# Fewer and larger loads near the end of a decode step: 29 load transfers in place of 37

## The chip, the cores and the metric

The kernel runs on one core of one Trainium2 chip. Its time is the device time of one execution in microseconds (us). The engines are named as in the profile: PE is TensorE (PEld its weight loads), DVE is VectorE, ACT is ScalarE, POOL is GpSimd, SP is SyncE, whose queue issues the loads.

## The reference: what is computed

One decode step of a transformer block for a single token, with modulated layer norms (`c` gives shifts, scales and gates), attention over a cache, and a feed-forward part with ReLU. Cut to what matters:

```python
D, Hq, Hkv, Sk, Dh, Dff = 512, 32, 8, 32768, 128, 1792       # bf16, one token
sa, ca, ga, sb, cb, gb = split(silu(c) @ w_mod, 6)
h = layernorm(x) * (1 + ca) + sa
q = h @ wq                                  # 32 query heads, 4 for each of 8 cached heads
p = softmax(q @ k.T / sqrt(Dh))             # over 32768 keys of each cached head
x = x + ga * ((p @ v) @ wo)
h = layernorm(x) * (1 + cb) + sb
out = x + gb * (relu(h @ w1) @ w2)
```

K and V of one cached head are 8 MiB each; eight heads make 128 MiB, all read once. The weights add wm (3 MiB), wq (4), wo (4), w1 and w2 (1.75 each).

## The kernel before, in words

**The stream.** All large loads go out on SP's queue, in the order of the list `stream`; `need(key)` issues the loads of the list up to the one that is wanted, and `load` makes one transfer of each entry. A load of K or V of head g is called Kg or Vg. Each is cut along the keys into four steps (0 to 3); a "half" is two steps. The order before is: half of K0, wm, wq, the other half of K0, then K1, V0, K2, V1, K3, V2, K4, V3, K5, V4 whole; K6 and V5 in halves; K7a, V6a, K7b, V6b (a and b are the first and the second half); V7 as a half and two quarters; wo in four pieces (`WOP`: four heads, two, one, one); w1 whole; w2 in five pieces (`W2P`). The second half of K0 is cut unevenly into three transfers (`UNEVEN`): 128 rows without their last 256 elements, and those 256 elements of 111 and of 17 rows.

**Room.** SBUF has a ring of three slots of 8 MiB each. A load takes the slot of the load three places back, so its issue waits until that one has been used: V6 for the scores of K6, V7 for PV of V5, wo and all that follows (`tail_sb`) for the scores of K7. SP's queue is in order: a load that waits holds up all behind it. Each transfer also waits for the one eight places before it, which used the same semaphore.

**One head.** For head h, `turn_k` transposes K on DVE in 32x32 blocks, `scores` multiplies it with the block-diagonal queries (`qbd`, 64 matmuls of 512 columns), and `softmax`, a generator that is advanced step by step with `next`, takes the maximum (DVE, PE), the exponentials (ACT), a transpose of P (DVE) and the sums (PE). `pv` multiplies P with V (64 matmuls of 512 columns, 16 a step), `blocks` (DVE), `o_cols` (PE) and `normalise` (DVE) bring the result into columns.

**The order of work.** PE and DVE follow the program's order (`manual_schedule`). In turn h of the loop stand the scores of head h, its softmax, and PV of head h-1. For heads 0 to 4 PV is a loop on PE; for later heads (`HALVED`) it is unrolled, and half of it may run before the softmax. Behind the loop comes head 7, written out by hand.

**The tail.** `spread(i)` lays the head outputs of piece i of wo out for `project(i)`. The first two pieces are multiplied row by row (`WOROWS`): one-row matmuls of 512 columns into `a_rows`, which `join_rows` turns into columns. The last two, of one head each, are multiplied as columns (L605). `keep_clock(n)` puts n matmuls in between whose result is not used. Then come the second layer norm (`layernorm_T`, whose result is `h2T`), w1 (L765), ReLU, w2 (L788), two DVE steps and the store.

`SPACE` is a number of drain instructions that SP executes after V0's load.

Of the kernel before, what the change touches and what calls it, by code (L numbers as in the profile page):

```python
# [17 lines left out]
def kernel(  # L18
# [25 lines left out]
    NTILE = Sk // (P * TK)  # L44
    NG = NTILE // 2

    WOP = [(0, Hkv // 2), (Hkv // 2, Hkv // 4), (Hkv - 2, 1), (Hkv - 1, 1)]
    WOROWS = 2
    LAST = Hkv - 1
    LOOPED = Hkv - 2  # L50
    HALVED = LOOPED - 1
    W2P = [(0, 5), (5, 10), (10, 12), (12, 13), (13, 14)]
    W1P = [(0, KT)]

    OUT0, OUT1 = 30, 34

    UNEVEN, EDGE, MOST = ("k", 0, (2, 3)), 2 * TK * Dh - D // 2, 111
    SPACE = 14
    assert Dh == 128 and REP == 4 and D == 512 and FT == W2P[-1][1] and NTILE == 4
    scale = float(Dh) ** -0.5  # L60
    eps = 1e-5
# [50 lines left out]
    def load(key):  # L112
        kind = key[0]
        if kind == "wm":
            t = piece("wmq_sb", 0, WM).rearrange("p (kt n) -> p kt n", kt=KT)
            src = wm_v
        elif kind == "wq":
            t = piece("wmq_sb", WM, WQ).rearrange("p (kt n) -> p kt n", kt=KT)
            src = wq_v
        elif kind in "kv":  # L120
            g, steps = key[1], key[2]
            src = (kv if kind == "k" else vv)[g, :, TK * steps[0]:TK * (steps[-1] + 1), :]
            name = f"Ksb{g}" if kind == "k" else f"Vsb{g}"
            t = piece(name, TK * Dh * steps[0], TK * Dh * len(steps)).rearrange("p (j d) -> p j d", d=Dh)
        elif kind == "wo":
            g0, n = WOP[key[1]]
            t = piece("tail_sb", g0 * REP * D, n * REP * D).rearrange("p (r d) -> p r d", d=D)
            src = wo_v(key[1])
        elif kind == "w1":
            k0, k1 = W1P[key[1]]  # L130
            t = piece("tail_sb", WO + k0 * Dff, (k1 - k0) * Dff).rearrange("p (kt f) -> p kt f", f=Dff)
            src = w1_v[:, k0:k1]
        else:
            f0, f1 = W2P[key[1]]
            t = piece("tail_sb", WO + KT * Dff + f0 * D, (f1 - f0) * D).rearrange("p (f d) -> p f d", d=D)
            src = w2_v[:, f0:f1]
        if key == UNEVEN:
            row, src_row = (x.rearrange("p j d -> p (j d)") for x in (t, src))
            for rows, cols in (
                (slice(0, P), slice(0, EDGE)), (slice(0, MOST), slice(EDGE, None)), (slice(MOST, P), slice(EDGE, None)),  # L140
            ):
                stream_dma(row[rows, cols], src_row[rows, cols])
        else:
            stream_dma(t, src)
        if key[:2] == ("v", 0):
            for _ in range(SPACE):
                nc.sync.drain()
        if kind in "kv":
            for i, u in enumerate(steps):
                loaded[(kind, g, u)] = t[:, TK * i:TK * (i + 1), :]  # L150
        else:
            loaded[key] = t

    def stream_dma(dst, src):
        i = nc.sync.dma_start(out=dst, in_=src)  # L155
        tc.stamp_issue_order_token(i.ins, "sp_stream")
        if last_loop:

            tc.add_manual_dep(i.ins, last_loop[0], mybir.DependencyInfo(
                mybir.DependencyClass.NoSync, mybir.DependencyReason.DATA))  # L160
# [1 line left out]
    whole, halves = [(0, 1, 2, 3)], [(0, 1), (2, 3)]  # L162
    stream = [("k", 0, halves[0]), ("wm",), ("wq",), ("k", 0, halves[1])]
    for g in range(LOOPED):
        stream += [("k", g + 1, s) for s in (halves if g >= HALVED else whole)] + [("v", g, s) for s in (halves if g >= HALVED else whole)]
    for s in halves:
        stream += [("k", LAST, s), ("v", LOOPED, s)]
    stream += [("v", LAST, (0, 1)), ("v", LAST, (2,)), ("v", LAST, (3,))] + [("wo", i) for i in range(len(WOP))]
    stream += [("w1", i) for i in range(len(W1P))] + [("w2", i) for i in range(len(W2P))]
    pos = [0]  # L170

# [71 lines left out]
    pick8 = const.tile([16, 8], BF16)  # L243
    nc.vector.tensor_tensor(out=pick8[:], in0=ident_bf[0:16, 0:8], in1=ident_bf[0:16, 8:16], op=ALU.add)
    cx_sel = const.tile([16, 2], BF16)
    nc.vector.tensor_copy(out=cx_sel[:], in_=cmask[8][0:16, 0:2])
    cx_bd = piece("wmq_sb", R0 + 2048 + 4 * P, D)[0:16].rearrange("p (b n) -> p b n", b=8)
    nc.vector.tensor_tensor(  # L248
        out=cx_bd, in0=cx_row[:].unsqueeze(1).to_broadcast([16, 8, D // 8]),
# [23 lines left out]
    def row_bank(t):  # L273

        nc.vector.memset(t, 0.0)
        return t
# [282 lines left out]
    def o_cols(g):  # L559
        nc.tensor.matmul(  # L560
            oT_ps[:, REP * g:REP * (g + 1)], lhsT=Y_tiles.pop(g)[:], rhs=qsel,
            start=True, stop=True, skip_group_check=True,
        )

    def part_of(g):
        return [i for i, (g0, n) in enumerate(WOP) if g0 <= g < g0 + n][0]

# [25 lines left out]
    def project(i):  # L593

        n = WOP[i][1] * REP
        wo_sb = need(("wo", i))
        for r in range(n):
            if i < WOROWS:
                nc.tensor.matmul(
                    a_rows[0][32 * (r % 4):32 * (r % 4) + 1, :], lhsT=o2_tiles[i][:, r:r + 1],  # L600
                    rhs=wo_sb[:, r, :], start=False, stop=(i == WOROWS - 1 and r >= n - 4), skip_group_check=True,
                )
                continue
            for ko in range(KT):
                nc.tensor.matmul(  # L605
                    attnT_ps[:, ko:ko + 1],
                    lhsT=wo_sb[:, r, :].rearrange("p (m ko) -> p ko m", ko=KT)[:, ko, :],
                    rhs=o2_tiles[i][:, r:r + 1], start=False, stop=(i == len(WOP) - 1 and r == n - 1),
                    skip_group_check=True,
                )  # L610

    a_rows = []

    def join_rows():

        aT = room("tail_sb", TAIL, [P, 512])
        nc.vector.transpose(
            out=aT.rearrange("p (a ko m) -> p a ko m", a=4, ko=KT),
            in_=a_rows[0].rearrange("p (a m ko) -> p a ko m", a=4, ko=KT),
        )  # L620
        for a in range(4):
            nc.tensor.matmul(
                attnT_ps[32 * a:32 * a + 32, :], lhsT=place32[:],
                rhs=aT.rearrange("p (a ko m) -> p a ko m", a=4, ko=KT)[:, a, :, 0],
                start=False, stop=False, skip_group_check=True,
            )

    spare = []
# [8 lines left out]
    with tc.manual_schedule(engines={mybir.EngineType.PE, mybir.EngineType.DVE}):  # L637
# [9 lines left out]
        for g in range(LOOPED):  # L647
            h = g + 1
            build_qbd(h)
            for u in range(NTILE):  # L650
                for half in range(2):
                    turn_k(h, u, half)
                    scores(h, u, half)
                if soft and u == 1:
                    next(soft, None)
            if g - 1 in [sum(w) for w in WOP]:
                spread(part_of(g - 2))
            if g >= HALVED:
                pv(g, (0, 1))
            soft = softmax(h)  # L660
            next(soft)
            if g > 0:
                blocks(g - 1)
            next(soft)
            if g > 0:
                o_cols(g - 1)
            next(soft)
            next(soft)
            pv(g, (2, 3) if g >= HALVED else (0, 1, 2, 3))
            if g > 0:  # L670
                normalise(g - 1)
            next(soft)
            open_o(h)
            next(soft)
        g, h = LOOPED, LAST
        build_qbd(h)
        turn_k(h, 0, 0)
        turn_k(h, 0, 1)
        next(soft, None)
        turn_k(h, 1, 0)  # L680
        turn_k(h, 1, 1)
        blocks(g - 1)
        scores(h, 0, 0)
        scores(h, 0, 1)
        scores(h, 1, 0)
        o_cols(g - 1)
        scores(h, 1, 1)
        normalise(g - 1)
        spread(part_of(g - 1))
        bank_max(h, 0)  # L690
        pv(g, (0, 1))
        for u in (2, 3):
            for half in range(2):
                turn_k(h, u, half)
                scores(h, u, half)
        bank_max(h, 1)
        soft = softmax(h)
        next(soft)
        next(soft)
        next(soft)  # L700
        pv(g, (2,), range(6))
        next(soft)
        next(soft)
        open_o(LAST)
        pv(g, (2,), range(6, 16))
        pv(g, (3,))
        next(soft)
        next(soft, None)
        end_b.append(two_banks("end_ps"))
        a_rows.append(row_bank(end_b[0][:, 0, :]))  # L710
        blocks(g)
        pv(LAST, (0, 1))
        o_cols(LAST - 1)
        normalise(LAST - 1)
        pv(LAST, (2,))
        spread(2)
        hid_ps = ps_o.tile([P, 512], F32, tag="o", name="hid_ps")
        nc.vector.memset(hid_ps[:], 0.0)
        pv(LAST, (3,))
# [3 lines left out]
        project(0)  # L723
        keep_clock(2)
        o_cols(LAST)
        keep_clock(2)
        project(1)
        normalise(LAST)
        spread(3)
        keep_clock(2)  # L730
        project(2)
        keep_clock(1)
        join_rows()
        keep_clock(1)
        project(3)


        stat2 = const.tile([P, 2], F32)
# [88 lines left out]
```

## Time and profile before

| | us |
|---|---|
| median of 3 runs | 354.13 (354.13 to 354.36) |
| the profiled execution | 354.42 |
| its span, first to last instruction | 352.6 |
| PE busy | 272.3 |
| DVE busy | 195.6 |
| mean load rate over the span | 424 GB/s |

In the profile a row of a timeline gives the start of a run of like instructions in us from the span's start, its length, the engine, the line of the kernel, the operation, what it writes and reads, how many there were, and in brackets how long the engine was idle before and what it waited for. A row of windows gives a stretch, its length, then busy time and number of instructions of PE, PEld, DVE, ACT and POOL, then PE's granted clock (1.00 is full), the share of the 16 DMA engines in use, and GB/s. A row of DMA issues gives how many transfers, their size, and the median time in us from issue to landing. The DMA queue of the loads is q1; its row has packets, MB and the share of the span of 16 engines.

### The profile page before, as it was taken

Reading aid. Unit: us, or ns where it says so; the run is one execution under the profiler, and the core shown is the slowest. Engines: PE = TensorE matmul, PEld = TensorE weight load, DVE = VectorE, ACT = ScalarE, POOL = GpSimd, SP = SyncE. Lnnn points to the kernel's source line nnn. Section 1 sums busy time; section 2 is a strip of 40 time slices with the busy share of each in tenths; the row PEclk is TensorE's granted clock in tenths of the full one; section 3 lists DMA queues with packets and bytes.
Section 4 is the critical chain, followed back from the end, with each engine's and each line's share of the span. In section 5 each row is a group of like instructions: output and inputs, shape, how many; then the busy total and the mean of one; then the engine's idle time right before and its main releaser. Section 6 shows DMA issues by size and latency. Waiting matters only on the chain. (4 is left out here: it accounts for less than half of the span.)

```text
span 352.6 us, 3544 instructions
## 1 busy us (share of the span) xinstructions
PE 272.3 (77%) x1310; PEld 111.8 (32%) x1310; DVE 195.6 (55%) x167; ACT 18.7 (5%) x37; POOL 6.0 (2%) x26
## 2 busy tenths in 40 slices
PE   0054980695999679884988499976999999789994
PEld 0021330232333224331333233322444443234442
DVE  7662563983079513965099316956674293743142
ACT  1200003001000010001000100001000100011000
POOL 3000000000000000000000000000000000000000
PEclk9996895698999969998999979996999999999999
DMA  8999989999999999999999999999999999999995
GB/s 353 404 432 456 468 387 461 446 401 446 439 424 440 416 439 446 401 455 446 409 453 446 409 453 431 426 394 439 446 414 427 450 429 424 431 453 398 432 426 213
DMA packets 5222, 149.57 MB, mean 424 GB/s; under 512 B 604, under 2 KB 988, under 8 KB 1628
## 3 DMA queue, kind: packets, MB, share of 16 engines
q1 hardware_dynamic: 5180, 149.43, 98.5%
q8 instruction: 8, 0.13, 0.1%
q14 instruction: 2, 0.02, 0.0%
q10 hardware_dynamic: 32, 0.00, 0.0%
HBM read 149.42 MB, written 0.00 MB: 424 GB/s over the span
## 5 line engine op out<-in xcount | busy, mean ns | idle before, releaser
L441 DVE STREAM_TRANSPOSE Ksb<-Ksb 128x4096 f32<-128x4096 f32 (+1 forms) x34 | 131.5, 3912 | 57.6 <-DMA Ksb<-in_A_k_cache_dram 57.6
L460 PE MATMUL S_ps<-Ksb,qbd 128*128 128x512 bf16 x512 | 118.9, 385 | 19.2 <-DVE Ksb L441 18.3
L523 PE MATMUL o_ps<-Vsb,P_g 128*16 (+1 forms) x512 | 124.3, 401 | 10.9 <-ACT P_g L497 10.0
L460 PEld LDWEIGHTS <-qbd 128*128 128x128 bf16 x512 | 49.2, 97 | 84.9 <-issue 27.6
L523 PEld LDWEIGHTS o_ps<-Vsb,P_g 128*16 x320 | 30.4, 95 | 60.0 <-issue 31.8
L523 PEld LDWEIGHTS <-P_g 128*16 128x16 bf16 x192 | 16.7, 90 | 22.9 <-issue 0.4
L473 DVE TENSOR_REDUCE m_p<-S_ps 128x1 f32<-128x1024 f32 x7 | 8.6, 1223 | 21.8 <-PE S_ps L460 21.8
L502 DVE STREAM_TRANSPOSE P_g<-P_g 128x1024 bf16<-128x1024 bf16 x8 | 10.0, 1245 | 15.6 <-ACT P_g L497 15.6
L494 ACT ACTIVATE nbias<-Mb_ps 128x1 f32<-128x1 f32 x8 | 1.4, 171 | 269.5 <-PE Mb_ps L492 269.5
L324 PE MATMUL mod_ps<-wmq_sb,siluT 128*1 128x512 bf16 x24 | 3.6, 624 | 9.9 <-DMA wmq_sb<-in_w_mod_dram 9.9
L332 DVE STREAM_TRANSPOSE Ksb<-Ksb 128x4096 f32<-128x4096 f32 x2 | 8.8, 4424 | 1.7 <-DMA Ksb<-in_A_k_cache_dram 1.7
L478 PE MATMUL mT_ps<-ident_f,m_p 128*1 128x128 f32 x8 | 2.2, 270 | 8.9 <-DVE m_p L473 7.9
L497 ACT ACTIVATE P_g<-S_ps,nbias 128x1024 bf16<-128x1024 f32 x8 | 8.9, 1114 | 0.2
L560 PE MATMUL acc_ps<-mask_sb,Y 16*128 16x4 f32 x16 | 3.4, 282 | 5.1 <-DVE Y L556 5.1
L552 DVE SCALAR_TENSOR_TENSOR o_ps<-o_ps,Linv,smask 16x512 f32<-16x512 f32 x8 | 5.8, 720 | 2.8 <-PE o_ps L523 2.8
L254 PE MATMUL xc_ps<-cx_sel,wmq_sb 16*128 16x2 bf16 x4 | 0.3, 172 | 8.7 <-DVE wmq_sb L248 8.7
L590 DVE CAST o_sb<-o_ps 128x4 bf16<-128x4 f32 (+2 forms) x4 | 0.7, 167 | 11.1 <-PE o_ps L586 11.1
L415 POOL TENSOR_TENSOR qbd<-qrep_sb,rowpick 128x64 bf16<-128x64 bf16 x8 | 2.4, 299 | 228.0 <-PE S_ps L460 198.3
L509 DVE RECIPROCAL Linv<-L_ps 16x1 f32<-16x1 f32 x8 | 1.0, 126 | 8.3 <-PE L_ps L506 8.3
L556 DVE TENSOR_REDUCE Y<-o_ps 16x128 f32<-16x512 f32 x8 | 5.4, 679 | 0.3
L635 PE MATMUL spare_ps<-qbd,ident_bf 128*128 128x512 bf16 x18 | 5.4, 381 | 0.0
L396 PE MATMUL q_ps<-wmq_sb,hT 128*1 128x512 bf16 x32 | 3.6, 626 | 2.3 <-DMA wmq_sb<-in_A_wq_dram 2.3
(114 smaller groups left out, 71.6 us busy)
## 6 DMA issues: line engine op xcount, KB each, us to landing
Ksb<-in_A_k_cache_dram SPq DMA_DIRECT2D x5, 4096.0 KB, 22.9
Vsb<-in_A_v_cache_dram SPq DMA_DIRECT2D x5, 4096.0 KB, 36.5
wmq_sb<-in_A_wq_dram SPq DMA_DIRECT2D x1, 4096.0 KB, 28.1
Vsb<-in_A_v_cache_dram SPq DMA_DIRECT2D x2, 2048.0 KB, 41.1
Ksb<-in_A_k_cache_dram SPq DMA_DIRECT2D x1, 4032.0 KB, 37.2
wmq_sb<-in_w_mod_dram SPq DMA_DIRECT2D x1, 3072.0 KB, 18.9
tail_sb<-in_A_wo_dram SPq DMA_DIRECT2D x1, 2048.0 KB, 23.2
tail_sb<-in_B_w_dram SPq DMA_DIRECT2D x1, 1792.0 KB, 30.6
```

The lines of the kernel that those rows point to most:

```text
L324: nc.tensor.matmul(dst[j // 4][32 * (j % 4):32 * (j % 4) + 1, :], lhsT=src_T[:, kt:kt + 1], rhs=w[:, kt, j * 512:(j + 1) * 512], start=(kt ...
L332: nc.vector.transpose(out=t, in_=t)
L396: nc.tensor.matmul(q_ps[i][32 * a:32 * a + 1, :].rearrange("o (h e) -> o h e", e=32), lhsT=hT[:, kt:kt + 1], rhs=wq_f[:, kt, i, a], start= ...
L441: t = nc.vector.transpose(out=KTt.bitcast(F32), in_=KTt.bitcast(F32))
L460: nc.tensor.matmul(S_ps_tiles[g], lhsT=qbd[g % 2][:, hp, 4 * (7 - s):4 * (7 - s) + P], rhs=KTv[:, 16 * sl:16 * sl + 16, h, :, par], start= ...
L473: behind_loop(nc.vector.reduce_max(out=m_p[:], in_=S_g.rearrange("p g f -> p (g f)"), axis=AX.X))
L497: nc.scalar.activation(out=P_g[:], in_=S_g.rearrange("p g f -> p (g f)"), func=ACT.Exp, bias=nbias[:], scale=scale, accum_out=l_g[:],)
L502: behind_loop(nc.vector.transpose(out=P_g[:], in_=P_g[:]))
L523: nc.tensor.matmul(o_tiles[g][:], lhsT=PT, rhs=Vx, start=first, stop=False, skip_group_check=True)
L552: nc.vector.scalar_tensor_tensor(out=o, in0=o, scalar=Linv_tiles.pop(g)[:], in1=smask[:].unsqueeze(2).to_broadcast([16, 4, Dh]), op0=ALU.m ...
L556: nc.vector.tensor_reduce(out=Y[:], in_=o.rearrange("p s d -> p d s"), op=ALU.add, axis=AX.X)
L635: nc.tensor.matmul(spare[0], lhsT=ident_bf[:], rhs=qbd[0][:, :, 0:P], start=True, stop=True)
```

## The change

- K0's second half is one transfer again (`UNEVEN`, `EDGE`, `MOST` are gone). SP executes four drains more after V0's load; in front of it two transfers are gone and two waits.
- K6 and V5 are loaded whole. After them come K7a, K7b, V6a, V6b, V7a, V7b, all halves.
- `build_qbd` of head 7 and the transposes of K7a move into the last turn of the loop, ahead of the transpose of head 6's P. Head 7's scores then come in one go, before any PV of head 6, and all PV of V6 comes behind them. `spread` of heads 4 and 5 falls away there.
- wo has two pieces of four heads, both multiplied by rows. So `spread` and `project` of the last four heads come after the last head's `normalise`, and `join_rows` is the last step of the projection. There are eight unused matmuls in this stretch, as before.
- w2 has four pieces: 6, 5, 2 and 1 of 14 instead of 5, 5, 2, 1 and 1.
- `cx_sel`, a small constant at the start, took its values from `cmask[8]`, which is no longer made; it now has a reduction of its own.

PE has 1923 rows of instructions in place of 1975, SP 29 loads in place of 37.

```diff
-    WOP = [(0, Hkv // 2), (Hkv // 2, Hkv // 4), (Hkv - 2, 1), (Hkv - 1, 1)]
-    WOROWS = 2
+    WOP = [(0, Hkv // 2), (Hkv // 2, Hkv // 2)]
-    W2P = [(0, 5), (5, 10), (10, 12), (12, 13), (13, 14)]
+    W2P = [(0, 6), (6, 11), (11, 13), (13, 14)]
-    UNEVEN, EDGE, MOST = ("k", 0, (2, 3)), 2 * TK * Dh - D // 2, 111
-    SPACE = 14
+    SPACE = 18
...
-        if key == UNEVEN:
-            row, src_row = (x.rearrange("p j d -> p (j d)") for x in (t, src))
-            for rows, cols in (
-                (slice(0, P), slice(0, EDGE)), (slice(0, MOST), slice(EDGE, None)), (slice(MOST, P), slice(EDGE, None)),
-            ):
-                stream_dma(row[rows, cols], src_row[rows, cols])
-        else:
-            stream_dma(t, src)
+        stream_dma(t, src)
...
     for g in range(LOOPED):
-        stream += [("k", g + 1, s) for s in (halves if g >= HALVED else whole)] + [("v", g, s) for s in (halves if g >= HALVED else whole)]
-    for s in halves:
-        stream += [("k", LAST, s), ("v", LOOPED, s)]
-    stream += [("v", LAST, (0, 1)), ("v", LAST, (2,)), ("v", LAST, (3,))] + [("wo", i) for i in range(len(WOP))]
+        stream += [("k", g + 1, whole[0]), ("v", g, whole[0])]
+    stream += [(x, g, s) for x, g in (("k", LAST), ("v", LOOPED), ("v", LAST)) for s in halves]
+    stream += [("wo", i) for i in range(len(WOP))]
...
+            if h == LOOPED:
+                build_qbd(LAST)
+                for u in (0, 1):
+                    for half in range(2):
+                        turn_k(LAST, u, half)
             next(soft)
             open_o(h)
             next(soft)
         g, h = LOOPED, LAST
-        build_qbd(h)
-        turn_k(h, 0, 0)
-        turn_k(h, 0, 1)
         next(soft, None)
-        turn_k(h, 1, 0)
-        turn_k(h, 1, 1)
-        blocks(g - 1)
-        scores(h, 0, 0)
-        scores(h, 0, 1)
-        scores(h, 1, 0)
-        o_cols(g - 1)
-        scores(h, 1, 1)
-        normalise(g - 1)
-        spread(part_of(g - 1))
-        bank_max(h, 0)
-        pv(g, (0, 1))
+        for u in (0, 1):
+            for half in range(2):
+                scores(h, u, half)
         for u in (2, 3):
             for half in range(2):
                 turn_k(h, u, half)
                 scores(h, u, half)
+        blocks(g - 1)
+        bank_max(h, 0)
         bank_max(h, 1)
         soft = softmax(h)
         next(soft)
         next(soft)
+        o_cols(g - 1)
+        normalise(g - 1)
         next(soft)
-        pv(g, (2,), range(6))
+        pv(g, (0,), range(6))
         next(soft)
         next(soft)
         open_o(LAST)
-        pv(g, (2,), range(6, 16))
-        pv(g, (3,))
+        pv(g, (0,), range(6, 16))
+        pv(g, (1,))
         next(soft)
         next(soft, None)
         end_b.append(two_banks("end_ps"))
         a_rows.append(row_bank(end_b[0][:, 0, :]))
+        pv(g, (2, 3))
         blocks(g)
         pv(LAST, (0, 1))
         o_cols(LAST - 1)
         normalise(LAST - 1)
         pv(LAST, (2,))
-        spread(2)
...
         project(0)
         keep_clock(2)
         o_cols(LAST)
+        normalise(LAST)
         keep_clock(2)
+        spread(1)
+        keep_clock(1)
         project(1)
-        normalise(LAST)
-        spread(3)
-        keep_clock(2)
-        project(2)
-        keep_clock(1)
+        keep_clock(3)
         join_rows()
-        keep_clock(1)
-        project(3)
```

More of the change, by code (lines that the diff above doesn't have):

```diff
@@ L245 @@
     cx_sel = const.tile([16, 2], BF16)
-    nc.vector.tensor_copy(out=cx_sel[:], in_=cmask[8][0:16, 0:2])
+    cx_half = const.tile([16, 2], F32)
+    nc.vector.tensor_reduce(
+        out=cx_half[:], in_=ident_f[0:16, 0:16].rearrange("p (c r) -> p c r", r=8), op=ALU.add, axis=AX.X,
+    )
+    nc.vector.tensor_copy(out=cx_sel[:], in_=cx_half[:])
     cx_bd = piece("wmq_sb", R0 + 2048 + 4 * P, D)[0:16].rearrange("p (b n) -> p b n", b=8)
@@ L597, in project @@
         for r in range(n):
[L598 to L610, printed above, removed]
+            nc.tensor.matmul(
+                a_rows[0][32 * (r % 4):32 * (r % 4) + 1, :], lhsT=o2_tiles[i][:, r:r + 1],
+                rhs=wo_sb[:, r, :], start=False, stop=(i == len(WOP) - 1 and r >= n - 4), skip_group_check=True,
+            )
     a_rows = []
@@ L624, in join_rows @@
                 rhs=aT.rearrange("p (a ko m) -> p a ko m", a=4, ko=KT)[:, a, :, 0],
-                start=False, stop=False, skip_group_check=True,
+                start=False, stop=True, skip_group_check=True,
             )
```

## The prediction

> **What bounds the kernel now.** Three views of the profile of before were read: the page (its slices, queues and chain), the chain of waits in order of time, and the timeline of the last 80 us. A letter after a head's number is a half of its load: V7b is steps 2 and 3 of V7.
>
> ```profile
> span 352.6 us, 3544 instructions
> ...
> q1 hardware_dynamic: 5180, 149.43, 98.5%
> ```
>
> The load queue (packets, MB, share) is busy for 98.5% of the span on all 16 engines, so 347.3 of 352.6 us. That is the bound: 149.4 MB in one unbroken stream. The end of the chain shows how little stands behind the stream:
>
> ```profile
> 338.50 11.12 DMA tail_sb<-in_B_w_dram
> ...
> 349.66 0.29 PE end_ps L788 x4
> ```
>
> The last piece of w2 lands at 349.62, four matmuls end at 349.95, and two DVE steps and the store follow. Whatever moves that landing moves the time one for one, as long as TensorE is ready for it. How ready it is, picked rows of the timeline show (start, length, engine, line):
>
> ```profile
> 272.87 15.49 SPq L155 DMA_DIRECT2D Vsb<-in_A_v_cache_dram  x4
> ...
> 313.77 0.27 PE L478 MATMUL mT_ps<-ident_f,m_p 128*1 128x128 f32 x1 [0.97 <-DVE m_p L475]
> 321.39 7.07 PE L523 MATMUL o_ps<-Vsb,P_g 128*16 128x512 bf16 x32
> 328.39 0.38 PE L560 MATMUL acc_ps<-mask_sb,Y 16*128 16x4 f32 x2
> 328.70 3.62 PE L523 MATMUL o_ps<-Vsb,P_g 128*16 128x512 bf16 x16
> 332.36 3.62 PE L523 MATMUL o_ps<-Vsb,P_g 128*16 128x512 bf16 x16
> 336.08 1.03 PE L599 MATMUL end_ps<-tail_sb,o_sb 128*1 128x512 bf16 x16
> 337.59 0.38 PE L560 MATMUL acc_ps<-mask_sb,Y 16*128 16x4 f32 x2
> 339.35 0.71 DVE L617 STREAM_TRANSPOSE tail_sb<-end_ps 128x512 f32<-128x512 f32 x1
> 341.71 0.16 DVE L740 TENSOR_TENSOR x1T<-acc_ps,modT_sb 128x4 f32<-128x4 f32 x1 [1.65 <-PE acc_ps L605]
> 343.74 0.22 DVE L307 SCALAR_TENSOR_TENSOR h2T<-cen_ln,rstd_ln,modT_sb 128x4 bf16<-128x4 f32 x1
> 345.33 0.93 PE L765 MATMUL hid_ps<-tail_sb,h2T 128*1 128x448 bf16 x16 [1.28 <-DMA tail_sb<-in_B_w_dram]
> 347.10 0.73 PE L788 MATMUL end_ps<-tail_sb 128*32 128x128 bf16 x20
> 348.30 1.64 PE L788 MATMUL end_ps<-tail_sb 128*32 128x128 bf16 x36 [0.47 <-DMA tail_sb<-in_B_w_dram]
> ```
>
> From 313.8 to 336 TensorE works without a pause through V6 and V7 (L523): it has a backlog, and each load is there before its turn. After it come the output projection, the second layer norm (h2T ready at 343.96) and a wait for w1, which lands at 345.2. So in the tail TensorE is 1.2 us ahead of the stream, and 0.5 us again at w2.
>
> **The change part by part.**
>
> *Fewer transfers.* Six joins (K6, V5, V7, two in wo, one in w2) take 9 packets each off every engine: 8 rows and a closing one. The price is bounded from two sides. Whole and split loads are compared where DVE takes a K as it lands:
>
> ```profile
> 98.87 4.45 DVE L441 STREAM_TRANSPOSE Ksb<-Ksb 128x4096 f32<-128x4096 f32 x1 [11.77 <-DMA Ksb<-in_A_k_cache_dram]
> 214.85 8.77 DVE L441 STREAM_TRANSPOSE Ksb<-Ksb 128x4096 f32<-128x4096 f32 x2 [10.74 <-DMA Ksb<-in_A_k_cache_dram]
> 243.99 8.77 DVE L441 STREAM_TRANSPOSE Ksb<-Ksb 128x4096 f32<-128x4096 f32 x2 [1.86 <-DMA Ksb<-in_A_k_cache_dram]
> 301.96 8.89 DVE L441 STREAM_TRANSPOSE Ksb<-Ksb 128x2048 f32<-128x2048 f32 x4 [5.83 <-DMA Ksb<-in_A_k_cache_dram]
> ```
>
> K2 to K5 are six whole loads in 115.98 us, 19.33 each; K6a to K7b are three loads in six halves in 57.97 us, 19.32 each. By that a join is worth nothing. On the other side, at the 432 GB/s of stretches whose DMA share is 1.00 (a row is below) the bytes need 345.9 us and the queue was busy 347.3; 1.4 us over 5180 packets on 16 engines is 4.3 ns a packet, 0.04 us a join, 0.25 us for six; twice that if the true peak is 433. I take 0.35 us, since the joins in wo and w2 are of small rows, where a packet's fixed part weighs most; the ends are 0 and 0.5. Nothing can be gained in idle time between transfers: 1.5% of the span covers the start and the end.
>
> *K0b unsplit.* Now 64 KB of it go as two thin pieces after the rest:
>
> ```profile
> Ksb<-in_A_k_cache_dram SPq DMA_DIRECT2D x1, 4032.0 KB, 37.2
> Ksb<-in_A_k_cache_dram SPq DMA_DIRECT2D x1, 55.5 KB
> Ksb<-in_A_k_cache_dram SPq DMA_DIRECT2D x1, 8.5 KB
> ```
>
> With 111 and 17 rows they can't be dealt to 16 engines as 128 rows are, so most engines are spared these bytes; 64 KB on all 16 are 0.15 us at 432 GB/s. The loss is 0 to 0.15 us, and I take 0.15, since the engines that end last are likelier to be spared ones. K0's own use has cover: K2, which takes its room, stands behind K1 and V0 in the stream. Stream in sum: -0.2 us (between +0.15 and -0.5); the last landing moves to 349.4, w1's to 345.0.
>
> *K6 and V5 whole.* At 9.66 us a half from K6a's 243.99 the stream gives K6 at 253.7, V5 at 273.0 and, in the new order, K7a 282.6, K7b 292.3, V6a 301.9, V6b 311.6. K6 is there only as a whole. Then four turns of 4.4 us and 16 matmuls end its scores as a steady head's end, 21.2 us after landing (K5: 214.85 to 236.05, next fence), at 274.9. Before, they ended at 272 with the row of 271.93; so PV of head 5 begins 3.3 us later, and K7's scores at 290.3 instead of 287.01. Behind them waits, on SP's queue, only V6's load: the stream is then busy with K7 until 292, 17 us of cover.
>
> ```profile
> 236.05 1.23 DVE L473 TENSOR_REDUCE m_p<-S_ps 128x1 f32<-128x1024 f32 x1 [3.73 <-PE S_ps L460]
> 271.93 7.07 PE L523 MATMUL o_ps<-Vsb,P_g 128*16 128x512 bf16 x32
> 287.01 5.39 PE L460 MATMUL S_ps<-Ksb,qbd 128*128 128x512 bf16 x24
> ```
>
> *Order K7, V6, V7; K7a turned early.* K7b lands at 292.3 instead of 301.96, and K7a is next to it. DVE turns K7a (four times 2.2 us, 282.7 to 291.6) ahead of head 6's P transpose, which waits there until 291.6; nobody needs it before V6a lands at 301.9. So K7's 64 scores are bound by TensorE: 290.3 to 304.1. Softmax runs as before (matmul of L478 at 305.1, and 7.8 us from it to the next whole PV, as 313.77 to 321.39 and one L560 more), and PV of V6b is done from 312.9 to 320.0. The tail's loads are issued at 304 instead of 312.83: no use, the stream is full till 331.
>
> *Where the backlog was, a wait comes.* V7b lands where V7's last quarter does now, at 331.15: the fourth issue of the row at 272.87 starts at 287.9 and takes 43.3 us (row below: one quarter 38.9, the median of both 41.1). V7a lands a half earlier, 9.67 us, at 321.4. So TensorE idles from 320.0 to 321.4, does V7a and L560 until 328.77, and idles again until 331.15: 2.4 us. Then all 32 matmuls of V7b are still to do, where now 16 of them are done by 332.3.
>
> ```profile
> Vsb<-in_A_v_cache_dram SPq DMA_DIRECT2D x1, 2048.0 KB, 38.9
> Vsb<-in_A_v_cache_dram SPq DMA_DIRECT2D x2, 2048.0 KB, 41.1
> ```
>
> At full clock V7b's PV ends at 331.19 + 7.07 = 338.26, against 335.98 now.
>
> *The tail behind it.* L560 1.6 us later (337.59 less 335.98), oA 0.7, spread and its cast 0.55, all 16 matmuls of wo's second half 1.03, one transpose 0.71, the joining matmuls and hand-overs 0.45: x1T 5.1 us after PV's end. It was 5.73; the column matmuls (L605) are gone. At full clock: x1T 343.36, h2T 2.25 later, w1's matmuls at 345.66, w2's 1.77 later at 347.43, and 56 of them at 36 ns and a 0.2 tail end at 349.66. The stream's end gives 349.4 + 0.33 = 349.75. So the 1.2 us of lead are used up, and from here every late us of TensorE counts in full.
>
> *The clock in the wait.* Is 2.4 us of idling enough to lose the clock? The granted clock changes only at steps of 3.41 us in this trace; stretches cut there (their first figures are length and TensorE's busy time, the last three clock, DMA share, GB/s):
>
> ```profile
> 119.29:122.70 3.41, 1.02 (x5) 0.21 (x3) 2.59 (x4) 0.00 (x0) 0.30 (x1) 1.00 0.93 404
> 122.70:126.11 3.41, 1.36 (x5) 0.94 (x6) 1.58 (x3) 1.38 (x3) 0.00 (x0) 0.50 1.15 500
> 156.83:160.25 3.42, 2.10 (x11) 0.76 (x9) 1.32 (x2) 0.00 (x0) 0.30 (x1) 1.00 1.10 479
> 160.25:163.66 3.41, 0.83 (x4) 0.47 (x4) 1.65 (x4) 1.35 (x3) 0.00 (x0) 1.00 0.93 404
> ...
> 310.43:313.84 3.41, 2.14 (x10) 0.73 (x8) 1.27 (x3) 0.00 (x0) 0.47 (x1) 1.00 1.07 461
> 313.84:317.25 3.41, 3.41 (x17) 1.33 (x18) 0.68 (x3) 1.58 (x4) 0.00 (x0) 1.00 1.00 432
> ```
>
> After the stretch with 1.02 us of matmuls the next runs at 0.50; after 2.10 or 2.14 it stays at 1.00. The border lies between. The new wait leaves 1.03 us busy when it falls inside one stretch, and then it decides like the row at 119.29. Where the stretches fall in another run I can't know: the wait is whole in one stretch in 30% of positions, and 1.7 us of it (half-way to the border's other end) in 70%. A halved stretch does 8 matmuls where 16 fit: 1.7 us lost, 1.3 if it starts before the wait ends; I take 1.6. The Trainium skill ("TensorE: Matmul & The Clock Gate", Why this matters for your kernels) says that idle gaps up to about 3 us keep the clock; the rows above do not agree, since the clock fell after gaps of 1.3 and 1.1 us in one stretch. By that rule the sum is the second case below.
>
> **Cases.**
>
> *Forecast, 55%: the clock halves before V7b's PV.* PV ends 339.86, x1T 344.96, w1 347.26, w2 349.03, its end 351.26: 1.3 us later than 349.95. The profiled execution took 354.42, with 1.8 around its span; it would take 355.7, and against the median of 354.13 that is 355.4. Its own range is 354.8 to 355.9.
>
> *Second, 33%: the clock holds,* as the gap is split over two stretches, or the first gap at 320.0 costs the clock early and V7a's slower PV fills the second. Then the stream bounds: -0.2 us, 353.9. For it: the border may lie near 1.02.
>
> *Other side, 8%: a transfer costs more than the rows show.* If each of the eight took 0.15 us, stream and V7b both come 1.0 us earlier, 353.1, and with the clock held it decides from 0.1 us a transfer on. Against it: 19.33 and 19.32.
>
> *The change starves the stream, 4%:* K6 in one piece delays V6's issue past K7b's landing. That needs 17 us more than reckoned; each us beyond adds one, say 356.
>
> Less than 0.2%, 0.7 us, can't be told from no change here. Of the first case a small part stays under that: faster 0.08, same 0.38, slower 0.54. The range 353.7 to 355.9 leaves out the third and fourth case.
>
> **What would show it.** In the changed kernel's timeline: L517 (L523 now) starting anew at about 321.4 and 331.15 with a wait for V7's DMA; PEclk 0.50 in a stretch that begins between 330.3 and 333; w1's matmuls no longer waiting for DMA; the end of the chain TensorE and DVE, not DMA. K7's scores without waits for DVE. I am wrong if the clock reads 1.00 there, if TensorE still has a backlog at 320 (then the stream bounds), or if the last w2 landing moves by more than 0.5 us.

## The result and the profile after

| | before | after |
|---|---|---|
| median, us | 354.19 | 354.94 |
| runs | 354.07 to 354.78 | 353.92 to 356.03 |
| profiled execution, its span | 354.42, 352.6 | 354.95, 353.1 |

The changed kernel takes 1.0019 times as long as the one before (95% interval 1.0012 to 1.0027). Its median hides two groups: 5 of 22 runs lie at 353.92 to 354.02, 17 at 354.56 to 356.03 with a middle of 355.2, and none in between. The profiled execution is of the upper group, near its lower end. The prediction was 355.4, with 353.9 for the case that the clock holds. Two runs of the kernel before, 361.92 and 363.88 us, are in a slower state that other kernels here show too; such runs are left out of the ranges and ratios, here and below.

The load queue and the shares of the chain that ended last, from the page of the changed kernel:

```profile
q1 hardware_dynamic: 4184, 149.42, 98.1%
...
DMA 21%; PE 10%; DVE 6%; issue 0%; SPq 0%; ACT 0%; ACTq 0%
```

The queue moves the same bytes in 996 packets less, and is still busy nearly all the time. But in this execution it no longer carries the end. The chain, in order of time (start, length, engine):

```profile
290.11 40.73 DMA Vsb<-in_A_v_cache_dram
330.84 0.04 issue
330.88 8.32 PE o_ps L517 x30
...
346.91 0.92 PE hid_ps L744 x16
...
348.63 1.76 PE end_ps L767 x54
```

The last DMA in it is V7b's load, which lands at 330.84; then PE and DVE, with one short step of ACT between w1 and w2, go on to the store. In the kernel before the last step was a DMA, the last piece of w2. The last w2 piece now lands at 349.11 in the trace (349.62 before) and finds PE still busy with earlier ones. Rows of the timeline that answer to those shown of before:

```profile
289.66 14.08 PE L454 MATMUL S_ps<-Ksb,qbd 128*128 128x512 bf16 x64
305.31 0.27 PE L472 MATMUL mT_ps<-ident_f,m_p 128*1 128x128 f32 x1 [1.57 <-DVE m_p L469]
305.82 1.57 PE L517 MATMUL o_ps<-Vsb,P_g 128*16 128x512 bf16 x6
307.52 7.21 PE L517 MATMUL o_ps<-Vsb,P_g 128*16 128x512 bf16 x26
314.62 13.97 PE L517 MATMUL o_ps<-Vsb,P_g 128*16 128x512 bf16 x64
330.88 8.32 PE L517 MATMUL o_ps<-Vsb,P_g 128*16 128x512 bf16 x30 [1.98 <-DMA Vsb<-in_A_v_cache_dram]
344.57 0.16 DVE L719 TENSOR_TENSOR x1T<-acc_ps,modT_sb 128x4 f32<-128x4 f32 x1 [0.37 <-PE acc_ps L607]
346.87 0.93 PE L744 MATMUL hid_ps<-tail_sb,h2T 128*1 128x448 bf16 x16
348.63 1.74 PE L767 MATMUL end_ps<-tail_sb 128*32 128x128 bf16 x56
```

K7's 64 scores come in one go. PE waits 1.98 us for V7b, and the 30 matmuls behind the wait take 8.32 us, where the same 30 at full clock take 6.63 (a row of the first experiment). w1's and w2's matmuls have no wait for a DMA any more. The clock, in stretches cut where it changes (length, busy time of PE, PEld, DVE, ACT, POOL, then granted clock, DMA share, GB/s):

```profile
303.62:307.04 3.42, 1.85 (x10) 0.83 (x9) 1.94 (x5) 0.00 (x0) 0.47 (x1) 1.00 0.91 393
307.04:310.45 3.41, 3.41 (x10) 1.11 (x9) 1.25 (x1) 2.66 (x4) 0.00 (x0) 0.50 1.05 452
...
327.52:330.93 3.41, 1.43 (x8) 0.70 (x7) 0.00 (x0) 0.00 (x0) 0.00 (x0) 1.00 0.96 413
330.93:334.35 3.42, 3.42 (x9) 1.12 (x9) 0.00 (x0) 0.00 (x0) 0.00 (x0) 0.50 1.01 431
```

The stretch with the wait for V7b has 1.43 us of matmuls, and the next one runs at half clock: 9 matmuls in it, where a full stretch at full clock holds 17 (the prediction's last row of windows). The same happened once earlier, at 307, behind the wait for head 7's maximum (1.57 us, the bracket of L472). This one was not foreseen.

### The profile page after: what moved, and what is told of

It reads as the page before. It is cut to its first block, busy times and chain, and to the rows that moved or that the text cites. A ratio compares the mean times of both kernels' runs of the same rounds, so it can differ in the third digit from the quotient of the medians.

```text
span 353.1 us, 3479 instructions
## 1 busy us (share of the span) xinstructions
PE 273.6 (77%) x1284; PEld 111.5 (32%) x1284; DVE 193.8 (55%) x160; ACT 18.7 (5%) x37; POOL 5.6 (2%) x24
## 5 line engine op out<-in xcount | busy, mean ns | idle before, releaser
L517 PE MATMUL o_ps<-Vsb,P_g 128*16 (+1 forms) x512 | 127.3, 409 | 12.8 <-ACT P_g L491 10.0
L517 PEld LDWEIGHTS <-P_g 128*16 128x16 bf16 x192 | 17.5, 93 | 27.3 <-issue 6.5
L472 PE MATMUL mT_ps<-ident_f,m_p 128*1 128x128 f32 x8 | 2.2, 270 | 9.5 <-DVE m_p L467 7.9
L475 DVE TENSOR_REDUCE Mrow<-mT_ps 1x4 f32<-1x128 f32 x8 | 2.2, 273 | 5.6 <-PE mT_ps L472 5.6
L500 PE MATMUL L_ps<-l_g,mask_sb 128*16 128x1 f32 x16 | 1.5, 165 | 4.5 <-ACT P_g L491 2.8
```

The source lines that it names most:

```text
L517: nc.tensor.matmul(o_tiles[g][:], lhsT=PT, rhs=Vx, start=first, stop=False, skip_group_check=True)
```

## Experiments

The theory: V7's last loads in halves leave PE without work, the clock halves in that wait, and PE then ends after the stream. Rivals: the transfers themselves (joins, K0's second half unsplit, K6 and V5 whole) move the time; or the late PV of V7b costs the same at full clock.

**The wait for V7b filled.** The changed kernel with seven matmuls in the wait, whose result is not used.

```diff
         normalise(LAST - 1)
+        keep_clock(7)
         pv(LAST, (2,))
```

> Changed kernel with seven unused matmuls (1.5 us) in the wait ahead of V7b's PV. Clock theory (the loss is the halved clock after the 2 us wait): PEclk stays 1.00 from 330 on, the upper group of times (354.6 to 356.0) disappears, the runs stand together at 353.9 to 354.1. Work theory (the loss is that twice the PV stands behind the last V landing, whatever the clock): still 354.9 in the median with the same spread. Stream theory (the loads are dealt worse to the DMA engines): still 354.9.

Measured: 354.31 (354.06 to 355.17), ratio to before 1.0004 (0.9995 to 1.0013). The profile of PE at the wait:

```profile
328.61 1.69 PE L620 MATMUL spare_ps<-qbd,ident_bf 128*128 128x512 bf16 x7
331.08 6.63 PE L517 MATMUL o_ps<-Vsb,P_g 128*16 128x512 bf16 x30 [0.79 <-DMA Vsb<-in_A_v_cache_dram]
...
345.39 0.93 PE L745 MATMUL hid_ps<-tail_sb,h2T 128*1 128x448 bf16 x16
...
347.16 0.84 PE L768 MATMUL end_ps<-tail_sb 128*32 128x128 bf16 x24
348.41 1.22 PE L768 MATMUL end_ps<-tail_sb 128*32 128x128 bf16 x32 [0.41 <-DMA tail_sb<-in_B_w_dram]
```

V7b comes no earlier (its PV starts 0.2 us later than in the changed kernel), but the 30 matmuls take 6.63 us, the clock is 1.00 there, w1 begins 1.48 us sooner, and the end waits for the stream again. Ten of the twelve runs lie at 354.06 to 354.60 and two above, 354.71 and 355.17; these two lie 2.4 us above their spans (352.3 and 352.8) where the others lie 1.8 to 1.9, so half a microsecond of theirs is outside the kernel's span. So the loss is the clock and not the late PV by itself; PV of the whole V7b fits ahead of the stream's end, with little to spare. But the runs do not come down to 353.9 to 354.1 as expected, nor to the changed kernel's lower group: their spans are 352.2 to 352.8, its lower group's 352.0 to 352.1. The last w2 piece lands at 349.31 in this trace and at 349.11 in the changed kernel's, with the same loads; why is not shown.

**All three waits filled.** As above, with 5 matmuls also in the wait for head 7's maximum and 3 ahead of V7a's PV.

```diff
         next(soft)
+        keep_clock(5)
         next(soft)
...
         blocks(g)
+        keep_clock(3)
         pv(LAST, (0, 1))
         o_cols(LAST - 1)
         normalise(LAST - 1)
+        keep_clock(7)
         pv(LAST, (2,))
```

> As the run before, and also five unused matmuls ahead of head 7's maximum (the wait at 303.7 to 305.3) and three ahead of V7a's PV. Clock theory: no stretch below 1.00 after 246; 353.9 to 354.0, at most 0.1 below the run that fills only the last wait, since the earlier halving at 307 only moves PV of V6 into the next wait. Work and stream theory: 354.9.

Measured: 354.36 (353.94 to 354.73), ratio 1.0003 (0.9994 to 1.0012). No gain over the one fill, and again 0.4 above what was expected; the spread is smaller, with nothing above 354.73. Filling the wait at 305 gains nothing that can be told: behind it PE still waits for V7a.

**V7 in halves alone.** The kernel before with V7b as one load instead of two quarters, and nothing else.

```diff
-    stream += [("v", LAST, (0, 1)), ("v", LAST, (2,)), ("v", LAST, (3,))] + ...
+    stream += [("v", LAST, (0, 1)), ("v", LAST, (2, 3))] + ...
```

> Kernel before with one part of the change alone: V7 in two halves. TensorE finishes V7a's PV at 328.8 as before and waits for V7b until 331.2, 2.4 us. Clock theory: two groups of times, about 354.2 with the clock held and 355.4 to 355.9 with it halved; median about 355.4. Work theory: one group at 354.2 to 354.7. Stream theory: 354.1, as nothing in the early stream is changed.

Measured: 354.53 and 354.74, then 355.81 to 355.97 (four runs); ratio 1.0037 (1.0024 to 1.0050). One joined transfer, with all others as before, gives the two groups. But the lower group, where the clock held (PEclk is full around the wait in the profiled run, 354.53), is still 0.3 to 0.5 us above the kernel before (354.23 beside it), which the clock does not explain. The same edit with one more drain on SP, for a reason given further down:

```diff
-    SPACE = 14
+    SPACE = 15
```

> The kernel before with V7 in two halves and one more drain in SyncE's program (15 for 14), so that its 80th instruction is again the wait for the output's landing, as in the kernel before. Position theory: 0.4 us of the V7-halves run's time came from an instruction of SyncE after the store that starts late wherever it stands 80th, and the rest from the clock. Then both groups of runs are 0.4 us lower than there: some at 354.0 to 354.3 (clock held), most at 355.2 to 355.6 (clock halved in the wait for V7's second half), median 355.4. Rival, nothing but the transfers and the clock counts: 355.85 as before, no run under 354.5.

Measured: 354.11 and 354.46, then 355.53 to 355.97 (four runs). The lower group is 0.3 to 0.4 lower than without the drain. The upper is 0.2 lower in its middle, its highest run no lower at all, and up to 0.4 above the band expected. The lower lies around the time of before (354.25 beside it), the upper 1.3 to 1.7 above it. The profiled execution is of the lower group. PE's rows and the clock around the wait:

```profile
330.82 3.61 PE L523 MATMUL o_ps<-Vsb,P_g 128*16 128x512 bf16 x16 [2.31 <-DMA Vsb<-in_A_v_cache_dram]
```

```profile
325.52:328.94 3.42, 2.99 (x15) 1.30 (x14) 0.29 (x1) 0.00 (x0) 0.00 (x0) 1.00 0.98 422
328.94:332.35 3.41, 1.53 (x8) 0.65 (x8) 0.00 (x0) 0.00 (x0) 0.00 (x0) 1.00 0.94 404
332.35:335.76 3.41, 3.41 (x17) 1.34 (x16) 0.65 (x2) 0.00 (x0) 0.00 (x0) 1.00 0.95 404
```

The wait is there in full, 2.31 us; the border of two stretches cuts it, 0.4 and 1.9 us, and the clock stays. So here the wait alone cost no time. No upper run of these two kernels was profiled; that the clock falls in them is inferred from the changed kernel's trace and the fill.

**V7b in quarters again.** The changed kernel with V7 as a half and two quarters.

```diff
-    stream += [(x, g, s) for x, g in (("k", LAST), ("v", LOOPED), ("v", LAST)) for s in halves]
+    stream += [(x, g, s) for x, g in (("k", LAST), ("v", LOOPED)) for s in halves]
+    stream += [("v", LAST, s) for s in ((0, 1), (2,), (3,))]
```

> Changed kernel with V7 as a half and two quarters again (30 loads). Its third step's PV starts at about 328.6 without a wait, V7's last quarter is done by 335.7, and the stream alone sets the end. Clock and work theory: 353.6 (last landing 349.1 in place of 349.62), all runs within 0.3. Stream theory: 354.9, as the stream is hardly changed.

Measured: 355.01 (354.58 to 355.45), ratio 1.0021 (1.0012 to 1.0030). A miss, by 1.4 us. PE's timeline, and the stretches around the new wait:

```profile
328.92 7.07 PE L518 MATMUL o_ps<-Vsb,P_g 128*16 128x512 bf16 x32
335.83 1.03 PE L593 MATMUL end_ps<-tail_sb,o_sb 128*1 128x512 bf16 x16
340.65 1.58 PE L593 MATMUL end_ps<-tail_sb,o_sb 128*1 128x512 bf16 x16 [1.92 <-DMA tail_sb<-in_A_wo_dram]
346.30 0.93 PE L745 MATMUL hid_ps<-tail_sb,h2T 128*1 128x448 bf16 x16
```

```profile
337.58:341.00 3.42, 1.50 (x14) 0.76 (x18) 0.47 (x2) 0.00 (x0) 0.00 (x0) 1.00 1.00 426
341.00:344.41 3.41, 3.41 (x29) 0.92 (x18) 1.14 (x7) 0.00 (x0) 0.00 (x0) 0.50 0.96 409
```

V7's PV is done at 336.0 as before, without a wait. But wo in two pieces brings the last four heads' rows whole, at 340.5; PE waits for them, and loses the clock there. So the wait had moved, from V7b's half to wo's half. It is at most a small part of the miss, though: the store of this run goes out at 350.48, sooner than in the kernel before (350.61), and the span ends 2.50 us after that, where it is 2.03 in the kernel before and 2.04 in the changed one. In the changed kernel PE arrives at wo's second half when it is already there, so this second trap lay behind the first.

That one filled too (eight unused matmuls for one before the last `project`):

```diff
         spread(1)
-        keep_clock(1)
+        keep_clock(8)
         project(1)
```

> Changed kernel with V7 as a half and two quarters, and eight unused matmuls in place of one ahead of the second project (the wait for wo's second piece, 338.7 to 340.65 in the run with the quarters). Clock theory: PEclk 1.00 to the end, w1's matmuls at 345.2 or earlier, 353.9 to 354.2, in one group. Work theory (what remains slow is that wo's second piece lands late and is worked off in one go): 354.8 or more, as nothing of that is changed.

Measured: 354.92 (354.47 to 355.21), ratio 1.0015 (1.0007 to 1.0024). A miss again, though the clock is 1.00 from 246 on and w2's matmuls end like those of before (349.93 against 349.95 in the traces). What is left lies behind them, in the ending: 2.49 us from the store to the end of the span.

**K0's second half unsplit, alone,** in the kernel before:

```diff
-    UNEVEN, EDGE, MOST = ("k", 0, (2, 3)), 2 * TK * Dh - D // 2, 111
-    SPACE = 14
+    UNEVEN, EDGE, MOST = None, 2 * TK * Dh - D // 2, 111
+    SPACE = 18
```

> Kernel before with one part of the change alone: K0's second half as one transfer, 18 drains. My estimate: most DMA engines carry 64 KB / 16 more, the last landing moves from 349.62 to about 349.75, 354.3. Rival: the thin pieces cost more than they save and the time falls by 0.2 or more.

Measured: 354.64 (354.31 to 355.02), ratio 1.0009 (1.0000 to 1.0018). The last w2 piece lands at 350.01 in its trace, 349.62 before. But the profiled execution is the slowest of the twelve, 355.02. At the median the whole difference is 0.35 us, and 0.18 of that is a longer ending (2.21 us against 2.03), which leaves 0.17 for the landing. And the uneven cut put back into the quartered and filled kernel, with 14 drains:

```diff
-    SPACE = 18
+    UNEVEN, EDGE, MOST = ("k", 0, (2, 3)), 2 * TK * Dh - D // 2, 111
+    SPACE = 14
...
-        stream_dma(t, src)
+        if key == UNEVEN:
+            ...
+        else:
+            stream_dma(t, src)
```

> As the run before, with K0's uneven cut and 14 drains put back. If the cut is worth 0.15 us to the engines that end last: 0.1 to 0.2 below the run before, about 353.9. If it is worth nothing: the same as the run before. This is the version that could beat both kernels.

Measured: 354.31 (354.18 to 354.47), ratio 1.0001 (0.9992 to 1.0010): 0.6 lower than without the cut, the last landing 349.25 against 349.60. The two pairs of traces give 0.35 to 0.4 us of landing for the cut. The endings give another 0.15 (2.34 us against 2.49); the two together are the 0.5 between the profiled executions (354.42 and 354.93).

**K6 and V5 whole, alone,** in the kernel before:

```diff
-        stream += [("k", g + 1, s) for s in (halves if g >= HALVED else whole)] + ...
+        stream += [("k", g + 1, whole[0]), ("v", g, whole[0])]
```

> Kernel before with one part of the change alone: K6 and V5 whole, 35 loads. Both theories: head 6's scores and all behind them come 3 us later on TensorE, still without a wait for the stream; the stream loses two joins: 354.0 to 354.2. If late scores of K6 hold up V6's load, the time rises instead and the load queue shows a gap near 275.

Measured: 354.73 (354.56 to 354.94), ratio 1.0012 (1.0003 to 1.0021), although its output is issued 0.4 us sooner than in the kernel before. Where the rest went, its SP rows tell, with the same edit with four more drains in the second fence:

```profile
core 0 of [0], span 352.9 us
...
350.20 0.29 SPq L796 DMA_DIRECT2D out_dram<-o_bf  x1
```

```diff
-    SPACE = 14
+    SPACE = 18
```

> The kernel before with K6 and V5 whole and four more drains in SyncE's program (18 for 14), so that its 80th instruction is the wait for the output's landing. Position theory: the output is issued at 350.2 as in the run of this edit without the drains (350.61 before), the span ends 2.0 to 2.2 us later as in the kernel before, at 352.2 to 352.4: 353.8 to 354.1. Rival, the joins themselves cost 0.4 us somewhere: 354.7 again.

```profile
core 0 of [0], span 352.4 us
...
350.21 0.29 SPq L796 DMA_DIRECT2D out_dram<-o_bf  x1
```

Measured: 354.23 (354.05 to 354.49), ratio 1.0000 (0.9991 to 1.0009). The store goes out at the same moment and the span ends 0.5 us sooner. Without that, the two joins cost nothing and gain nothing that can be told. The span ends at 352.4, inside the 352.2 to 352.4 expected; 354.23 is over the 353.8 to 354.1 expected because the time lies 1.8 us above the span (354.17 and 352.4 in the profiled execution), where 1.6 to 1.7 had been added. The last piece lands 0.4 us sooner than in the trace of before (349.23 and 349.62), and 0.15 of that goes into a longer ending (2.18 us against 2.03).

**The ending by itself.** The kernel before with two drains fewer on SP, and no other edit:

```diff
-    SPACE = 14
+    SPACE = 12
```

> The kernel before with 12 drains for 14 in SyncE's program and nothing else, so that the instruction that stands 80th is the drain behind the wait for the output's landing and no longer lies under that wait. Position theory: the output is issued at 350.6 as before and the span ends 2.4 us later for 2.0: 354.6, +0.4. Rival, endings differ for another reason: 354.2, no change.

Measured: 354.74 (354.56 to 354.99), ratio 1.0013 (1.0004 to 1.0022). SP's rows, first of the kernel before and then of this one, each with its drains in the ending (count, shortest, middle and longest in ns):

```profile
core 0 of [0], span 352.6 us
...
350.61 0.29 SPq L796 DMA_DIRECT2D out_dram<-o_bf  x1
```

```profile
L822 SPq DRAIN  x3: 7/7/7, 351.9 to 352.2; - x3
```

```profile
core 0 of [0], span 352.9 us
...
350.39 0.29 SPq L796 DMA_DIRECT2D out_dram<-o_bf  x1
```

```profile
L822 SPq DRAIN  x3: 7/7/123, 352.0 to 352.5; - x3
```

2.5 us from the store's issue to the end of the span instead of 2.0, and one of the three drains took 123 ns where all three take 7 before. This drain is SP's 80th instruction. It follows the wait for the output's landing, 0.45 us behind it in the trace. In the kernel before the 80th is a wait that stands ahead of the output's landing and is over before it, so nothing shows.

**The best parts together.** The changed kernel with the fill ahead of V7b, K0's uneven cut, and 25 drains.

```diff
-    SPACE = 18
+    UNEVEN, EDGE, MOST = ("k", 0, (2, 3)), 2 * TK * Dh - D // 2, 111
+    SPACE = 25
...
         normalise(LAST - 1)
+        keep_clock(7)
         pv(LAST, (2,))
```

> The changed kernel with seven matmuls on idle data in the wait for V7's second half (their result is not used), K0's second half cut unevenly as in the kernel before (31 loads), and 25 drains, so that SyncE's 80th instruction is the wait for the output's landing. Clock 1.00 to the end; the last w2 piece lands 0.3 us earlier than in the filled kernel without the cut, which took 354.31. With 31 loads the output's landing is the first of SyncE's six last waits, the others come after it at 0.06 us each, 0.3 us: 354.1 (353.9 to 354.3). If the cut's 0.35 us all count and the order of the waits costs nothing: 353.9. If the clock is lost again: 355 and a second group.

Measured: 354.39 (354.20 to 354.63), ratio 1.0003 (0.9994 to 1.0012). No better than the kernel before, nor than the fill alone (354.31). The last landing is at 349.23, only 0.08 before that of the fill alone (349.31), where 0.3 was expected; the ending takes 2.35 us from the store on (350.22 to 352.57) against 2.03 there (350.30 to 352.33), and these 0.3 had been reckoned. The expected 1.00 clock to the end was missed once, at 306, behind the wait for head 7's maximum; it did not bring an upper group, so that halving is free here too.

## Why the prediction was right, and where it was off

*The forecast case came true in 17 of 22 runs, the second in 5.* That the time splits in two, at about 353.9 and 355.4, is the main reading, and the fills and the lone joined load show the cause. 55 to 33 leaned the right way, but too little: 17 of 22 is 77%. The last full stretch of the trace of before (347.98 to 351.39, 1.58 us of matmuls, half clock behind it) would have put the border at 1.58 to 2.10 us in place of 1.02 to 2.10; an estimate by the prediction's own way, for its wait of 2.4 us, is then that 63 to 94% of positions lose the clock.

*Of its signs of being wrong, two of three appeared.* PE had a backlog at 320: matmuls run from 314.62 to 328.59 without a pause. And the last w2 landing moved by 0.51 us, where more than 0.5 was the sign. Neither overturned the case. The backlog came from clock lost at 307 and was used up before V7b landed; the landing moved forward, as forecast, only further. The third sign, a clock of 1.00 behind V7b, did not appear.

*K6 and V5 whole, the new order, K7a early: right.* K7's scores start at 289.66 (290.3 forecast), end at 303.7 (304.1), in one piece. The 0.6 us between is a slip of the sum: scores that end at 274.9 in place of 272 are 2.9 us later and not 3.3; K7's scores started 2.65 later than before. Nothing of it reaches the end, as the joins of K6 and V5 alone show.

*The waits: one of three was overlooked.* The prediction had PE busy from 290.3 to 320.0 and named waits at 320.0 and 328.77. Its own figures hold a third: scores end at 304.1 and the matmul of L478 follows at 305.1, like the 0.97 us in the row of 313.77, but this was not weighed for the clock. The wait is 1.57 us, since both reductions for head 7's maximum (1.29 us on DVE) now follow the last score, where one (0.69) did before. In the profiled run that wait halved the clock from 307.04 on. It slowed V6's PV (26 matmuls in 7.21 us; 5.78 in the filled run), which filled the wait for V7a, and V7's PV then started without a pause. The second case had put an early loss of clock among the ways in which the clock holds at V7b, as V7a's slower PV would fill the wait. Here the loss came earlier than it had in mind, the clock was full again from 310.45 on, and V7a's PV was not slowed. V7b's wait shrank to 1.98 us, from 2.4 forecast, and the clock fell all the same.

*The halving: right in size.* 8.32 us less 6.63 for the 30 matmuls is 1.7; the step took 1.6. V7's PV ends at 339.63, forecast 339.86.

*The tail: one term mis-sized.* x1T comes 4.94 us after PV's end (5.1), w1's matmuls 2.30 after x1T, w2's 1.76 after w1's. But the 56 matmuls of w2 take 1.74 us, with the hand-over 1.76, where the sum had 36 ns each and a tail of 0.2, 2.23. The prediction does not say where its 36 ns come from; the row of before that it shows, 20 in 0.73 us, gives 36.5, but in it the time that the last matmul takes to end is already counted. Rows of 20 in 0.73, 24 in 0.84 and 56 in 1.74 us fit 28 ns for each and 0.17 once, so the tail was counted twice. So the matmuls end at 350.39 and not at 351.26; 0.5 us of this is the w2 term, 0.2 the earlier V7b, 0.15 the shorter step to x1T. Against the 349.95 of before that is 0.44 us, and the profiled execution is 0.53 slower than the profiled one of before. The upper group as a whole is 1.0 above before's median; 1.3 had been forecast. The 1.8 us around the span were carried over, and were right by luck: the ending is 2.04 us from the store here and 2.03 before, but 2.50 in the quartered kernel with one load more, and the prediction had not asked what sets it.

*The stream: mis-sized, its terms not well known.* Its last landing moved by 0.5 us in the profiled run (0.3 with the fill) against 0.2 forecast. K0 unsplit costs 0.35 to 0.4 us of landing in two pairs of traces and 0.08 in a third; worked out from the medians less the endings, the same pairs give 0.17, 0.46 and 0.24. The prediction's upper bound was 0.15, which priced the 64 KB at the mean rate. By the single traces the six joins are then worth 0.4 to 0.9, and not 0.35 (its working with 433 GB/s gives 0.4 and not twice 0.25); K6 and V5 alone moved the landing to 349.22 and 349.23. Single traces of like streams lie 0.2 to 0.3 apart (349.62 and 349.40 for the loads of before), so neither term is known better than that. The two errors cancel in part, so it is partly luck that the lower group lies near the 353.9 forecast. In the upper group none of it decides, since there the stream is not the end. That a landing moves the time one for one holds only where the ending stays as long: K6 and V5 alone landed 0.4 us sooner and took 0.4 longer.

*The rivals.* Transfers that cost 0.15 us each would have given 353.1: the landings came some way towards it, but PE ended later than the stream. That K6 in one piece starves the stream did not happen. The rule of the Trainium skill ("TensorE: Matmul & The Clock Gate", Why this matters for your kernels) that gaps up to about 3 us keep the clock would have made 353.9 the one result; waits of 1.57 and 1.98 us lost it here, one of 2.31 us kept it.

*What stays open.* Why single upper runs are as low as 354.56, and which of the two or three waits halved in each, can't be told without a trace of each. The two highest, 355.67 and 356.03, lie 2.3 to 2.4 us above their spans in place of 1.8 to 1.9, and what that is isn't known. Why the filled kernels stay 0.3 us above the lower group is open too.

## What to carry to other kernels

When a load is made larger near the end of a stream, ask first what its consumer does until the whole of it has landed: the bytes come no later, but the first part comes only with the last, and an engine that had a backlog gets a pause. On PE a pause can cost twice, itself and then the clock, and matmuls of no use put into it can keep the clock; here that won back 0.6 us and no more than the time of before. When a row of like instructions is turned into a time for each, take the last one's own duration out first, and when two kernels differ by a few tenths, look at the time between the output's issue and the end of the span before explaining it by anything else.

## What the runs showed of the hardware

**The clock can fall after waits of 1.6 to 2 us, and not by busy time alone.** Over the traces of all 14 kernels here, each cut in its stretches of 3.41 us, every stretch from 60 us on at full clock with less than 1.5 us of matmuls was followed by half clock, and none with more than 1.9. In between both occur. The same stretch as at 303.62 above, in the first filled kernel, kept it:

```profile
302.26:305.67 3.41, 1.84 (x9) 0.61 (x7) 2.01 (x4) 0.00 (x0) 0.47 (x1) 1.00 1.04 452
305.67:309.09 3.42, 3.42 (x18) 1.57 (x18) 0.51 (x3) 1.41 (x4) 0.00 (x0) 1.00 1.06 460
```

What decides between 1.5 and 1.9 us wasn't found. The prediction's border, between 1.02 and 2.10, holds.

**The place of an instruction in SP's program costs up to 0.5 us.** Counted in the traces without branches, SP's 80th instruction starts some 0.4 us late in every kernel looked at where nothing else is waited for there: a drain behind the landing in the shifted kernel (2.5 us from store to end for 2.0), in K6 and V5 whole (2.7; 2.2 after four drains more, both fences above), a wait behind the landing in V7 in halves (2.5; 2.1 after one drain more), and the last drain in the two quartered kernels of 30 loads. With 86 instructions in the kernel before it is over before the output's landing; with 80 in the changed one it is the very last, and costs 0.05. In all 14 traces queue q14, which the page calls an instruction queue, moves one block of 8 KB 0.4 to 0.9 us after the 80th has started. So the place goes with the loading of instructions; but this transfer comes behind the late instruction, and why that one is late isn't shown. It means that a change in the number of loads, by shifting SP's program, can move a time by as much as the edits tested here.

**The order of the last waits counts too.** SP ends with six waits, for the DMAs' semaphores among others, one after another at 0.06 to 0.08 us each. With 37 or 29 loads the output's landing is the last of them; with 31 or 32 it is the first, and the other five come behind it. That is the 0.3 us by which the ending of the last experiment (2.35 us) is longer than that of the first (2.03).
